# Half 0's frequency products in one piece, the router's input by transposing loads, and table 1's sine arguments on TensorE

## The chip, the cores and the metric

The kernel runs on one core of a Trainium2 chip. Its time is the device time of that core in microseconds (us), as the median of several runs. The engines are called as in the profile: PE (TensorE, matmuls), DVE (VectorE), ACT (ScalarE), POOL (GpSimd) and SP (SyncE, which issues most DMAs).

## The reference

For a sequence `x` of 2048 tokens and 512 channels the reference mixes a long convolution (branch a) and a small expert (branch b) with a gate per token:

```python
g = sigmoid((x * gate_w).sum(-1, keepdims=True))
a = _A_ref(x, A_re, A_im, B_re, B_im, C_re, C_im, log_dt, Dskip)
b = _B_ref(x, w_r, w_gate, w_up, w_down)
return g * a + (1 - g) * b

# _A_ref: a state space model as a convolution of length 2048
dt = exp(log_dt)[:, None]; logdA = dt * (A_re + 1j * A_im); dB = dt * Bc
l = arange(L).astype(bfloat16)
P = exp(logdA[:, :, None] * l)                      # 512 x 128 x 2048
K = einsum("dn,dnl,dn->dl", Cc, P, dB).real         # the kernel, 512 x 2048
y = irfft(rfft(K, padded) * rfft(u, padded))[:L] + u * Dskip

# _B_ref: the two tokens with the largest r get an expert's output
r = x @ w_r;  idx = argsort(-r)[:2]
y = (silu(x[idx] @ w_gate) * (x[idx] @ w_up)) @ w_down * sigmoid(r[idx])
return x + scatter(y at idx)
```

Inputs and output are bf16.

## The kernel before

**The method.** The lags `l` are rounded to bf16, so fewer distinct lags occur than there are tokens. The powers `P` are split in two tables of complex exponentials, table 1 (coarse lags, `tab1`) and table 2 (fine lags, `tab2`, with the weights folded in: the products r0 to r3). A matmul of the two over the 128 states gives the distinct values of the kernel (`kgen`, L920), selector matmuls sort them (`sel`, L933 to L949), and a matmul with constant matrices kp0 to kp4 turns them into the kernel's spectrum kk (`kspec`, L975). The sequence is cut in two blocks of 1024 tokens (0 and 1). A forward transform by matmuls with constant matrices f0 to f3 gives each block's spectrum X (`forward`, L896, evicted at L901; POOL's accumulating DMAs, L906, add the pairs `pm`). DVE multiplies spectra (`products`): block 1 of the output is X1*K0 + X0*K1, block 0 is X0*K0. The matrix g brings them back (`inverse`, L1057), and ACT or DVE scale the result by the gate and store it (L1068, L1072).

**Halves.** The 512 channels are worked on in two halves (h = 0, 1) of 256. Tables, kgen, kspec, products and inverse are done for each half, the forward transform once for both.

**Table 1's sines.** For a group g of up to four angles, `trig` scales the phase b16 once for each angle to a 32-bit integer tile `arg` (`SCL`, L477), takes the sine of its low 16 bits on ACT (`AC`, L463), adds a quarter turn to the tile (L667, DVE or ACT), and takes the sine again. Groups 0 and 1 have four angles, group 2 has two and gets the rest by doubling formulas, group 3 has none of its own.

**The router** (`routing`). Eight groups of eight transposes on PE (L766) bring u, 128 tokens by 128 channels at a time, to channel-major tiles xt0 to xt3, evicted by ACT or DVE through `EV` (L467). 64 matmuls with the gate's and the router's weights (L781) give the logits; four rounds of reductions (L796, L800) find the two largest; a gather matmul (L828), the expert's matmuls (L849, L863) and a small transpose (L870) follow. The result row zby is added to a copy of u in the output by an indirect DMA on POOL (L874), and u is loaded back from there before the inverse. xt lies where block 1's X comes later; w_down is loaded over xt once the logits are done.

**Products.** For a half, `products` is called four times: block 1 then 0, and in each the two halves of the frequencies (`qds` is (0,) or (1,)). A call makes one (block 0) or two (block 1) products of 4096 columns, adds them, and forms real and imaginary parts and the sum and difference over `pm` with pieces of 1024 columns, into X. The products lie in 8 KB tiles of the pools pqa, pqb, pqc and pqd.

**Order.** Nothing is scheduled at run time. Every operation has a number in the order in which the program states it. The string ORDER lists these numbers in the order in which they are put on their engines' queues; SECOND says for each operation that two engines can do which of them does it; PLACES gives PSUM banks and tiles. Each engine works its queue in order and waits by semaphores for what an operation reads or overwrites. DMAs of SP's queue are likewise in order: an issue that waits holds the ones behind it. ACT holds one of two function tables at a time; a change is a load of 1.28 us (L220).

**Places that matter here.** kp0 to kp3 lie over f0 to f3, so each can be loaded when the forward transform has used its f for the last time; kp4 lies behind them and is loaded near the start.

Of the kernel before, what the change touches and what calls it, by code (L numbers as in the profile page):

```python
# [10 lines left out]
F32 = mybir.dt.float32  # L11
# [342 lines left out]
def small_mats():  # L354
# [15 lines left out]
POOLS = {"pqa": 1, "pqb": 1, "pqc": 2, "pqd": 2}  # L370
ORDER = (
    "00k00500201601501l00000100300700d00h00i00400900600800u00g00e00c00j00f00n00l00m08e00o00p00q00s00r00t01g01d01e01h00x00y00z01c01801704003x04104801a01b03z"
    "04a03y01003v02502604900w00v01x01v01101208g04b01w01r01z04201y02002302402102701t05g01u04504301s02202804c01304604402902a02j02k05h03w02l02m02n01402o06k06j"
    "04d05i02p04e04705m05j02q02r05k05n01q04f02s03401o01p02b01j01m01i01902c01n01f02t06s02u03702v06r04i02w02x02y03802z06p03004j03103204l03303904k03c04g04m03d"
    "04h03i06l03a03504n06m08f04o03g03b06q06n06o04p03j04q05o04r03h02d04u04s03m06x06y04t06z07002e01k04w07107204y03n04v08i06t08j04z04x06u07300a03l07403k03o00b"
    "03p05007607505p08l05405305q06v06w05l07807706703q06605108v07907a08k05r05u05t05207c08m03r08s06808n08t03s03603t07d07b08u05507i07h07g07f07e07l07k06906a05v"
    "07j05905a05605b05c05x08w08h06b08x05d05708z08o05e05w05y08y08p09009t09v07m07p07n07o07q08q09o08r09107r09309n07s07t09207v02g09407u09p09w09509602h09709807z"
    "07y09q09u08107w09r09s0a10a20a308207x09x09y06c06d06005z0a40a50a60a80a70aa0a906e09z08c0a00ac0ab0ad0ae06g06f06108a06208d06308009a09905806h08308409b06402f"
    "08509e08603e09g03f0af08708b0ag0ai09c0aq0ah05s03u05f06506i09d0am09i09f0ar0b00b209j0880b10as0an0ak0aj0b30al0at0b70b80b90b40b50b60ax0ay0au0av09h09k0ap0ao"
    "09l09m0az0ba0be02i0c50890cd0bd0bb0bg0bh0aw0c60cc0c70c30c20c10bc0bk0bj0c00bi0bf0bl0dk0bm0bn0bp0bo0bq0dl0dh0bt0bu0br0bs0by0di0ce0c80bv0bw0cf0bx0d30d40cg"  # L380
    "0ct0c90c40ch0co0ca0dd0dg0bz0cv0cu0df0de0d50dj0ci0cb0cw0d00et0cj0dn0d60cq0cx0cp0d10d20do0dt0cy0cz0cl0eu0ck0d70du0da0dr0dp0dm0dq0d80dx0cr0d90e80db0dc0cm"
    "0cn0f30f40dv0ey0ez0dw0cs0ds0e40e70ea0ev0ew0e90ef0e30eb0ed0eh0el0ex0fs0f00fv0f50f10e50fo0e60fu0fr0fn0em0f70f60f20ec0eg0en0ee0ej0ft0fw0fx0fz0f80eo0g00g5"
    "0ek0ei0f90gh0fq0fp0fy0g30gi0fa0fb0fc0fd0g10ge0gd0g60gj0g70gl0dy0gf0gg0gk0gn0g80fe0gm0go0gq0g20g40dz0gp0ff0fg0fi0gr0fh0fj0h00gv0fm0fl0gw0gx0gy0fk0es0gs"
    "0gt0gu0er0ep0eq0e00gb0ga0gc0e20g90h10e10h90gz0ha0h40h50h60h20h70hb0h30h80hc"
)
SECOND = (
    "000000000000000000000000000000000000100000000000000000000000000000101010100010100000100100000000000000000000000000100010000000000000000000000010010001"
    "000110010100001010010010011010000000000000000000000000000000000000000000000000000000001010010010100000100000000000000000000000000000000000000000000000"
    "000001000001010000000100000110100000100100000000101000000010000010000000000000000000000000000000000000000000000000000000000000000000000000000000000000"
    "000000000000000000000000000000000000000000000000000000000000000000000000000000000000000000000000000000000000000000000000000000000000000000000000000000"  # L390
    "0000000000010011000100000"
)
PLACES = (
    "2406154064740000000020660011001266446040110064604014001100111016606022026424242200101026264262451016541026000171234265"
)
KB = 1024


def bass_gated_mix__ssm_conv_s4__moe_arch_mod__prompt_kernel(nc, A_u, A_A_re, A_A_im, A_B_re, A_B_im, A_C_re, A_C_im, A_log_dt, A_Dskip,
# [22 lines left out]
    with ExitStack() as es:  # L422
# [145 lines left out]
        for i in range(2, 6):  # L568
            prm_l(i, eng=ACT if i % 2 else SP)
# [583 lines left out]
```

## Time and profile before

| | |
|---|---|
| median of 3 runs (lowest to highest) | 153.71 us (153.7 to 154.03) |
| the profiled execution's own time | 153.72 us |
| its span, first to last instruction | 151.9 us |
| mean granted clock of PE | 0.955 |
| busy: PE, DVE, ACT, POOL | 129.7, 138.2, 131.1, 24.8 us |
| weight loads on PE | 96.4 us |
| DMA | 24.09 MB, mean 159 GB/s |
| start of kgen(0) on PE | 58.3 us after the span's start |
| start of kspec(0) on PE | 81.6 us |
| first product on DVE | 93.2 us |
| last matmul ends | 148.3 us |

Times within the span count from its start. "Busy" counts an engine's instructions from start to end, and neighbours overlap by some 0.09 us on DVE and ACT, so the cost of one more instruction in a full queue is its time from start to start, a little less than its mean duration. A row of a group gives line, engine, operation, shapes, how often it runs, its busy time and mean duration, and the idle time just before, with what ended it. A helper's line (L452, L467, L477) collects the operations of the whole kernel.

### The profile page before, as it was taken

To read this page: it belongs to the slowest core of one execution; us is meant where nothing else is said; L and a number is where in the kernel's file an instruction comes from. 1 tells how busy PE (TensorE), PEld (TensorE's weight loads), DVE (VectorE), ACT (ScalarE), POOL (GpSimd) and SP (SyncE) were. 2 spreads that over 40 slices of the span, in tenths; PEclk is the share of its full clock that TensorE was granted. 3 is DMA by queue.
4 is the path that set the end of the run, shared out by engine and by line. 5 is a ranking of instruction groups with operands and counts; after the bars stand their busy time and mean duration, and the time that the engine had idled before them with its cause. 6 is when DMAs were issued, how large, how long until landed. Compare 5 with 4: busy or idle time off the path is not lost.

```text
span 151.9 us, 3786 instructions
## 1 busy us (share of the span) xinstructions
PE 129.7 (85%) x1605; PEld 96.4 (63%) x1613; DVE 138.2 (91%) x199; ACT 131.1 (86%) x218; POOL 24.8 (16%) x17
## 2 busy tenths in 40 slices
PE   0974787467989986979996999997999999999990
PEld 0944542464354336973454787995888867888880
DVE  0499999999999999999999974999999999999961
ACT  3599999999999999999999569397599999999731
POOL 3000001000122999910055000001000000000000
PEclk9999999955699999999997799999999999999999
DMA  5999999939908604000389997006800001014154
GB/s 136 344 293 388 414 403 404 350 108 330 365 2 119 162 0 138 4 5 0 92 231 254 275 275 118 6 4 203 356 0 2 4 2 35 0 54 123 35 173 138
DMA packets 14546, 24.09 MB, mean 159 GB/s; under 512 B 1175, under 2 KB 10146, under 8 KB 14370
## 3 DMA queue, kind: packets, MB, share of 16 engines
q1 hardware_dynamic: 11410, 21.11, 40.8%
q0 software_dynamic: 2144, 2.10, 9.0%
q10 hardware_dynamic: 976, 0.66, 1.6%
q8 instruction: 12, 0.20, 0.5%
q14 instruction: 4, 0.03, 0.1%
HBM read 19.66 MB, written 4.20 MB: 157 GB/s over the span
## 4 chain that ended last, share of the span: by engine, by line
PE 53%; DVE 28%; ACT 8%; DMA 6%; issue 3%; SPq 0%; ACTq 0%
PE ps L1057 18%; DVE AR L452 18%; PE ps L975 13%; PE ps L920 11%; DMA AR<-c_ksp 4%; DVE AR L467 3%; ACT AR L463 3%; PE ps L896 2%; PE ps L1010 2%; DVE AR L477 2%; ACT AR L467 2%; ACT AR L667 2%; DMA AR<-c_bf 2%; DVE AR L456 1%; PE ps L933 1%
## 5 line engine op out<-in xcount | busy, mean ns | idle before, releaser
L452 DVE TENSOR_TENSOR AR<-AR 128x1024 bf16<-128x1024 bf16 (+8 forms) x129 | 115.6, 952 | 7.2 <-DMA AR<-c_bf 3.8
L467 ACT ACTIVATE AR<-ps 128x1024 bf16<-128x1024 f32 (+10 forms) x45 | 35.0, 807 | 9.1 <-PE ps L975 4.7
L896 PE MATMUL ps<-AR 128*128 128x512 bf16 x122 | 31.0, 405 | 3.2 <-ACT AR L901 1.5
L1057 PE MATMUL ps<-AR 128*128 128x256 bf16 x256 | 29.5, 273 | 0.0
L1057 PEld LDWEIGHTS ps<-AR 128*128 128x128 bf16 x256 | 25.0, 98 | 3.1
L896 PEld LDWEIGHTS ps<-AR 128*128 128x128 bf16 x128 | 12.5, 104 | 18.9 <-issue 3.6
L975 PE MATMUL ps<-AR 128*128 128x256 bf16 x160 | 20.8, 288 | 1.3 <-DMA AR<-c_ksp 1.3
L975 PEld LDWEIGHTS ps<-AR 128*128 128x128 bf16 x160 | 16.4, 103 | 5.3 <-DMA AR<-c_ksp 1.6
L920 PE MATMUL ps<-AR 128*128 128x84 bf16 (+1 forms) x512 | 17.9, 196 | 1.7 <-DVE AR L452 1.7
L920 PEld LDWEIGHTS ps<-AR 128*128 128x128 bf16 x512 | 17.8, 96 | 2.2 <-ACT AR L463 2.2
L463 ACT ACTIVATE AR<-AR 128x1024 bf16<-128x1024 int16 (+5 forms) x24 | 18.5, 773 | 0.5 <-DVE AR L477 0.3
L463 ACT ACTIVATE ps<-AR 128x256 f32<-128x256 bf16 (+1 forms) x36 | 18.0, 549 | 0.1
L874 POOL DMA_INDIRECT out_dram<-AR x1 | 16.2, 16210 | 2.8 <-ACT AR L477 2.8
L901 ACT ACTIVATE AR<-ps 128x1024 bf16<-128x1024 f32 x16 | 15.9, 1015 | 0.0
L1068 ACT ACTIVATE AR<-ps,AR 128x256 bf16<-128x256 f32 x28 | 11.4, 482 | 4.3 <-PE ps L1057 3.4
L477 ACT ACTIVATE AR<-AR 128x256 int32<-128x256 f32 (+2 forms) x28 | 13.8, 518 | 0.0
L463 ACT ACTIVATE AR<-ps 128x512 bf16<-128x512 f32 (+1 forms) x18 | 11.9, 757 | 2.0 <-PE ps L597 2.0
L906 POOL DMA_DIRECT2D AR<-AR x4 | 5.3, 1464 | 17.6 <-ACT AR L901 16.0
L667 ACT ACTIVATE AR<-AR 128x1024 int32<-128x1024 int32 (+1 forms) x9 | 7.8, 867 | 0.1
L766 PE MATMUL ps<-AR 128*128 128x128 bf16 x64 | 4.6, 220 | 3.2 <-DVE AR L452 1.4
L477 DVE TENSOR_SCALAR AR<-AR 128x256 int32<-128x256 f32 (+2 forms) x20 | 6.5, 336 | 0.0
L766 PEld LDWEIGHTS ps<-AR 128*128 128x128 bf16 x64 | 3.6, 98 | 4.3 <-DVE AR L467 2.0
(67 smaller groups left out, 91.3 us busy)
## 6 DMA issues: line engine op xcount, KB each, us to landing
AR<-c_ksp SPq DMA_DIRECT2D x5, 512.0 KB, 3.9
AR<-in_A_u_dram SPq DMA_DIRECT2D x4, 512.0 KB, 5.5
AR<-c_fwd SPq DMA_DIRECT2D x4, 512.0 KB, 7.9
AR<-AR POOLq DMA_DIRECT2D x4, 512.0 KB, 12.9
AR<-out_dram SPq DMA_DIRECT2D x4, 512.0 KB, 10.1
AR<-c_inv SPq DMA_DIRECT2D x1, 2048.0 KB, 8.8
AR<-in_B_w_up_dram SPq DMA_DIRECT2D x1, 1792.0 KB, 12.0
AR<-in_B_w_gate_dram SPq DMA_DIRECT2D x1, 1792.0 KB, 16.1
```

The lines of the kernel that those rows point to most:

```text
L452: return P.op(DVE, lambda h: h.tensor_tensor(out=o, in0=a, in1=b, op=op), rd, wr, cost=cst or tt_cost(o, a, b), **k)
L463: return P.op(ACT, lambda h: h.activation(out=o, in_=a, func=func, scale=scale, bias=bias), rd, wr, cost=0.185 + nel(o) * 0.833e-3 + (0.09 ...
L467: return P.op((ACT, DVE), (lambda h: h.activation(out=o, in_=a, func=ACTF.Copy), lambda h: h.tensor_copy(o, a)), rd, wr, cost=(0.185 + n * ...
L477: return P.op((ACT, DVE), (lambda h: h.activation(out=o, in_=a, func=ACTF.Copy, scale=c), lambda h: h.tensor_scalar(out=o, in0=a, scalar1= ...
L667: P.op((DVE, ACT), (lambda hh: hh.tensor_scalar(out=w, in0=w, scalar1=16384.0, scalar2=None, op0=ALU.add), lambda hh: hh.activation(out=w, ...
L874: P.op(POOL, lambda h: h.indirect_dma_start(dr(out, 0, (D, L), (1, D)), bass.IndirectOffsetOnAxis(ap=IDX(0, 2, 0, (1, 1)), axis=0), ZB(0, ...
L896: last = h.matmul(pb(0, 128, part * 512, (1, 512)), F[ft](0, 128, ((par * 4 + st) * 2 + part) * 128, (1, 128)), U(0, 128, (blk * 8 + st * ...
L901: P.op((ACT, DVE), (lambda hh, o=o, i_=i_, sc=sc: hh.activation(out=o, in_=i_, func=ACTF.Copy, scale=sc), lambda hh, o=o, i_=i_, sc=sc: hh ...
L920: last = hh.matmul(pb(0, 128, g // 6 * 512 + g % 6 * W4 + o, (1, n)), TP[h][1 - i // 2](0, 128, (b0 + g) * 128, (1, 128)), r[i](0, 128, (b ...
L975: last = hh.matmul(pb(0, 128, n * 256, (1, 256)), KP[u](0, 128, tau * 128, (1, 128)), KC[h](0, 128, jg * 256, (1, 256)), start=(k == 0 and ...
L1057: r = hh.matmul(pb(0, 128, e * 256, (1, 256)), G(0, 128, ((par * 2 + part) * 4 + ft) * 512 + (2 * t2 + e) * 128, (1, 128)), X(0, 128, blk ...
L1068: r = hh.activation(out=U(0, 128, tb * D + h * HC, (1, HC)), in_=pb(0, 128, e * 256, (1, HC)), func=ACTF.Copy, scale=SG(0, 128, 64 + tb, ( ...
```

## The change

- **Router input.** The eight transposes and their evictions go. Four DMAs on SP's queue load 128 channels each of u for all 2048 tokens, transposed on the way (`transpose=True`), straight into xt0 to xt3. The tokens now lie in their natural order, so the logit matmuls take every second column.
- **Table 1's sine arguments.** A new constant `an` (164 KB) holds the angles' multipliers, spread so that a matmul picks a channel's phase and multiplies it. The phases, reduced to one turn's fraction, are split on DVE (and for one step ACT or DVE) into two bf16 tiles pa0 and pa1. `angles` takes the place of `trig` in `tab1`: for each PSUM bank PE adds a rounding constant (512 columns), then eight matmuls of 128 columns written with stride 4; ACT takes the sine of the low 16 bits in PSUM; PE adds a quarter turn with one more matmul of 512 columns; ACT takes the second sine. Groups 0 and 1 need two banks each, group 2 one.
- **Places.** an, pa0 and pa1 lie where kp4 comes later, so kp4 is loaded after the last angles of half 1.
- **Products.** For half 0, `products` is called with both halves of the frequencies at once: two calls in place of four, with products of 8192 columns in 16 KB tiles (pools pqa and pqc with two units). Half 1 is as before.
- **New order.** ORDER, SECOND and PLACES are new. Read number by number: SP issues the parameters, `an`, the four transposing loads, then u's first quarter, f2, u's second quarter, f1, f3, u's other quarters, w_gate, w_up, half of w_down, the rest of the small constants, the other half, f0; later kp0, kp2, kp3, kp1, kp4 and the reloads of u. On PE the angles of groups 0 and 1 come first, then the logits, the angles of group 2, and the forward transform mixed with the router; half 1's angles of groups 0 and 1 stand between the expert's matmuls, its group 2 in the end of the forward transform. All four accumulating DMAs stand behind the indirect one on POOL. The last eviction of kgen(1) goes from ACT to DVE, behind the second product of half 0. Several other operations change engine or place.

```diff
-POOLS = {"pqa": 1, "pqb": 1, "pqc": 2, "pqd": 2}
+POOLS = {"pqa": 2, "pqc": 2, "pqd": 2}
...
+def angle_mats():
+    out = np.zeros((128, 642))
+    c = 0
+    for g in range(4):
+        j0 = DBL1.get(g, (4, 0, 0, 0))[0]
+        ts = [a // 8 for a in ANG1[4 * g:4 * g + j0]]
+        for i, t in enumerate(ts):
+            for p in range(128):
+                out[p, c + p % 64 * j0 + i] = t
+        c += 64 * j0
+    out[:, 640], out[:, 641] = 1.5 * 2.0 ** 23, 16384.0
+    return out
...
+        AN = B("an", oF + 16 * KB, 2 * 642)
+        PA = [B("pa%d" % i, oF + 16 * KB + 1536 + i * KB, 1 * KB) for i in range(2)]
...
+        DQ([(AN(0, 128, 0, (1, 642)), an_c[:, :])], [], [AN], 164352)
...
+        for db in range(4):
+            P.op(SP, lambda h, db=db: [h.dma_start(XT[db](0, 128, 0, (1, L)), dr(A_u, db * 128, (D, L), (1, 128)), transpose=True)], [], [XT[db]], cost=0.5, nbytes=786432, dma=True)
...
+        TS(DTC(0, 128, 0, (1, 4)), DTP(0, 128, 0, (1, 4)), -8.0 * c16, ALU.mult, [DTP], [DTC])
+        TT(XR[0](0, 128, 0, (128, 4), (1, 128)), PRM(0, 128, D, (128, 4), (1, 128)), DTC(0, 128, 0, (1, 4), (0, 128)), ALU.mult, [(PRM, 1), DTC], [XR[0]])
+        TS(f512(XR[1]), f512(XR[0]), MG, ALU.add, [XR[0]], [XR[1]])
+        STT(f512(XR[2]), f512(XR[1]), MG, f512(XR[0]), ALU.subtract, ALU.subtract, [XR[0], XR[1]], [XR[2]])
+        EV(f512(PA[0]), f512(XR[2]), [XR[2]], [PA[0]])
+        TT(f512(PA[1]), f512(XR[2]), f512(PA[0]), ALU.subtract, [XR[2], PA[0]], [PA[1]])
...
+        def angles(h, g, ts):
...
+            def add(hh, col, first):
+                for b in range(nb_):
+                    r = hh.matmul(pb(0, 128, b * 512, (1, w)), IDN(0, (1, 128)), AN(0, 128, col, (0, w)), start=first, stop=False, skip_group_check=True)
+                return r
+            def ang(hh):
+                add(hh, 640, True)
+                for x in range(2):
+                    for k in range(4):
+                        for b in range(nb_):
+                            r = hh.matmul(pb(0, 128, b * 512 + k, (4, w // 4)), PA[x](64 * h, 64, k * 128, (1, 128)), AN(64 * h, 64, c0 + b * (w // 4), (1, w // 4)),
+                                          start=False, stop=False, skip_group_check=True)
+                return r
+            so = lambda k: s(0, 128, k * 4 * HC, (16, 64), (1, 4 * na_))
+            P.op(PE, ang, [CBI, AN, *PA], [pb], cost=nb_ * (0.2157 + 8 * 0.1))
+            AC(so(0), lo, ACTF.Sin, [pb], [(s, "s")], scale=SC16, tset=ts)
+            P.op(PE, lambda hh: add(hh, 641, False), [CBI, AN], [pb], cost=nb_ * 0.2157)
+            AC(so(2), lo, ACTF.Sin, [pb], [(s, "c")], scale=SC16, tset=ts)
...
-                s = made[g] = trig(h, ANG1[4 * g:4 * g + j0], ts[g // 2], True, "1%d%d" % (h, g), 4) if j0 else place("snc", TRG, oI + 8 * KB, 6 * KB)
+                s = made[g] = angles(h, g, ts[g // 2]) if j0 else place("snc", TRG, oI + 8 * KB, 6 * KB)
...
-            for q in range(8):
-                bb = misc(True)
-                def tr(h, q=q, bb=bb):
...
-                P.op(PE, tr, uk(2 * q, 2 * q + 1) + [CBI], [bb], cost=0.455)
-                EV(XT[0](0, 128, q * 256, (2 * L, 2), (L, 2), (1, 256)), bb(0, 128, 0, (512, 2), (256, 2), (1, 256)), [bb], [(XT[i], q) for i in range(4)])
...
-                                last = h.matmul(b(0, 128, tb * 2, (1, 2)), XT[db](0, 128, tb * 128, (1, 128)), WL(0, 128, db, (4, 2)), start=(db == 0), stop=(db == 3))
+                                last = h.matmul(b(0, 128, tb * 2, (1, 2)), XT[db](0, 128, j * 1024 + st * 256 + par, (2, 128)), WL(0, 128, db, (4, 2)), start=(db == 0), stop=(db == 3))
...
-            for qd in range(2):
-                products(0, (qd,), (blk,))
+            for qds in (((0, 1),) if blk in (1, 0) else ((0,), (1,))):
+                products(0, qds, (blk,))
```

74 lines of the change are left out of this document (41 added, 33 removed).

## The prediction

> **What bounds the kernel now.** I read the slices first, to see which engine is full where, then the chain that ended last, then PE's and DVE's instructions in order of time, then the groups by shape for prices.
>
> The slices (one digit is 3.8 us):
>
> ```profile
> PE   0974787467989986979996999997999999999990
> DVE  0499999999999999999999974999999999999961
> ACT  3599999999999999999999569397599999999731
> PEclk9999999955699999999997799999999999999999
> DMA  5999999939908604000389997006800001014154
> ```
>
> DVE and ACT are full up to about 80 us while PE has gaps; from about 94 us PE and DVE are both full. PE's clock is halved once, around 31 to 41 us, and the DMA engines are full up to about 35 us. The chain, in its pieces:
>
> ```profile
> 50.44 7.76 DVE AR L452 x7
> ...
> 58.33 8.96 PE ps L920 x256
> ...
> 75.47 6.10 DMA AR<-c_ksp
> ...
> 81.61 8.83 PE ps L975 x64
> ...
> 107.22 7.09 PE ps L975 x64
> ```
>
> DVE builds half 0's table 2 until 58.2; PE then makes half 0's kernel (kgen, L920) until 67.3, finishes the forward transform at 75.45, and frees the forward matrix f1; kp1 is loaded over it (6.1 us); kspec(0) (L975) starts at 81.6, and from there PE runs almost without a gap to 148.3. So the end moves with the start of kspec(0), unless the products on DVE fall behind. PE before that, and the one long wait of DVE:
>
> ```profile
> 16.36 0.62 PE L766 MATMUL ps<-AR 128*128 128x128 bf16 x8
> 17.67 0.81 PE L896 MATMUL ps<-AR 128*128 128x512 bf16 x3 [0.69 <-DVE AR L467]
> 18.32 1.74 PE L781 MATMUL ps<-AR 128*128 128x2 bf16 x64
> 58.33 8.95 PE L920 MATMUL ps<-AR 128*128 128x84 bf16 x256 [1.73 <-DVE AR L452]
> 93.19 2.29 DVE L452 TENSOR_TENSOR AR<-AR 128x4096 bf16<-128x4096 bf16 x1 [2.92 <-DMA AR<-AR]
> ```
>
> Before kgen(0) PE waits for DVE; the products start at 93.2 when the accumulating DMA of block 1's X has landed.
>
> **Time base.** The profiled execution took 153.72 us, its span is 151.9, so 1.8 us lie around it; the median of the runs is 153.71, the same. A difference of 0.2% (0.3 us) is about what a measurement of this kernel tells from none.
>
> **Part 1, router input by transposing loads.** Removed: 64 transposes on PE (L766 back to back, 56 ns from start to start: 3.6 us), six evictions on DVE (0.69 us each, 0.60 from start to start: 3.6) and two on ACT (1.01, 0.95: 1.9). Added: four loads of 512 KB on SP's queue, ahead of u and the forward matrices. Their price is in no row, as no load here transposes. Lower bound: a plain 512 KB load, 1.35 us each when the loads stream (f2 lands at 12.58, u's next quarter at 13.93). By packets: a source row is 256 bytes, and packets of 256 bytes took 18 ns (136 of them) against 84 ns for 2048; 8192 packets of 18 ns on 16 engines are 9.2 us, 2.3 each. Upper end: the slowest 512 KB transfers of the trace, the accumulating ones, 5 us each when they share the engines. I take 2.3, since packet size is the property that a row shows; the loads would then land at about 14.5 (5.3, when the parameters and the angle constants are in, plus 9.2). SP issues nothing else meanwhile if it is held.
>
> The Trainium skill (VectorE: DVE Perf Modes, "The three transpose paths") gives the DMA path 1309 ns for a 128x128 block against 390 on TensorE, and tells authors to use TensorE where PSUM will do: it speaks against this part. An estimate from that figure: 64 blocks one after another 84 us, spread over 16 engines 5.2; no run here shows it.
>
> What waits: the logits (L781) stand in PE's new order behind the parameters' matmuls and the first angles, before any forward matmul, so a late landing stops PE. Behind the loads, u's quarters and f1 to f3 land 9.2 us later than they could, then w_gate (28.8 by sums of 4.7 us per 1.8 MB) and w_up (33.5), then w_down (38.7). In the new order PE comes to their matmuls at 30.6, 34.8 and 40.8, so some 2 us are spare.
>
> **Part 2, sine arguments by PE.** Removed: 20 scalings (5 on DVE at 0.28 us, 0.20 from start to start; 15 on ACT at 0.42, 0.33) and 6 quarter-turn adds (DVE 0.60; ACT 3 x 0.95 + 2 x 0.54): DVE -1.6, ACT -8.9. Added on DVE, once: a tiny scale, two arithmetic steps of 0.60, one of 0.36, a cast of about 0.45, a subtraction of 0.60: +2.7. Added on PE, per PSUM bank: two 512-column matmuls (0.216) and eight of 128 columns written with stride 4, as L597 writes (0.109 from start to start at full clock): 1.30 us; five banks per half, ten in all: 13.0. The sines themselves keep their size; ACT reads PSUM at the pace of SBUF (1042 against 1055 ns for 1024 columns).
>
> Sum of both parts, with the ops that change engine: DVE -2, ACT -11, PE +9.4. The load goes from the two full engines to the one that has gaps.
>
> **Where PE then stands.** From 10.0 to 58.3 PE was busy 37.2 us, 8.4 of it at half clock (4.2 at full). At full clock the same work is 33.0. New ahead of kgen(0) are half 0's five banks (6.5) and four banks of half 1 (5.2), gone are the transposes (3.6): +8.1, so 41.1. Waits along the new order, for sines, for the router's reductions on DVE and for eviction, add 3 to 6: kgen(0) starts at 54.4 to 57, I take 55.7. DVE's work up to its last table-2 product sums to 52.5, and the expert's result row (zby, waiting for dn at 42.4 and its transposes) holds it up about 2.5: 55.0. So the two meet, and kgen(0) starts 2.6 us earlier than 58.3. From there to the end of the forward transform is 17.1 as now plus the last angle group (1.1), less a little waiting: 73.7 instead of 75.45. kp1's landing (6.1, or some 5.0 by the selector matmuls that run meanwhile if kp4's later issue leaves kp1 freer) puts kspec(0) at 78.7 to 79.8: 2.3 us gained.
>
> kp4 moves from the first loads (it landed at 26.6) to behind kp1, since the angle constants lie in its place. Its 0.5 MB now runs beside the accumulating DMAs; kspec needs it 4.4 us after its start, by when it is in. POOL has all four accumulating DMAs behind the scatter now, with a memset among them; only one ran early before.
>
> **Part 3, products of half 0 in one piece.** 24 DVE instructions become 12 of twice the size: 12 fixed parts of 0.06 us (0.59 from start to start for 1024 columns, less 1024 x 0.523 ns) are 0.7 us of DVE. The price is order: the first product needs all of block 1's X and all four kk0 tiles (90.4 with kspec(0) at 79.8), where now one pair of kk0 tiles and half an X suffice. The accumulating DMAs move about 100 packets of 1 KB per us beside loads, 5.1 us for 512; from 75.5 the third lands near 91.5. So the products start at 91.5 instead of 93.2, the first 16 KB product takes 4.35 (2.285 + 4096 x 0.523 ns, less overlap). The last kgen(1) eviction is DVE's now, after the second product: at 101.5, no later than PE needs it. PE waits 1.0 us less there than now (1.4 at 102.2), of which I count 0.5. The inverse of half 0 then finds its X (pm add 109.8, pm sub 110.9) as PE gets there (110.9).
>
> **Sum.** -2.3 at kspec(0), -0.5 in the selector: 153.7 - 2.8 = **150.9 us**. By the ends of the waits, 148.9 to 153.
>
> **Rivals.**
> *Late transposes (slower).* From 16.5 us on, every us by which the transposed input lands later goes into PE's start, and from some 2 us beyond 14.5 also into w_up, w_down and zby. At 5 us per load they land at 25.3, 8.8 late: 159.7; halfway between my price and that (3.65) at 19.9: 154.3. For it: nothing in the trace bounds the write side of a transposing load; against: the packet sizes. No gain is left from a landing at 19.3 on (16.5 and the 2.8).
> *The accumulating DMAs decide.* Four of them, kp4 and the reloads of u share the engines from 73.7. For it: they ended DVE's wait at 93.2; against: the first is issued earlier now. If X of block 1 lands at 95 and that of block 0 at 100, the second product ends at 104.5, the eviction behind it holds the selector to 105, and the gain is lost: 153.7 to 154.5.
> *PE is not the bound (faster).* For it: PE had 11 us of gaps between 10 and 58.3; against: the sum above fills them. If PE's waits hide and DVE's saved 5.5 us (r3's last product 57.7 to 52.5) come through: 148.2.
> *The clock.* In the new order PE has only two short adds and the logits between 14.4 and 18.5. If the clock halves there for 10 us as it did from 30.7 to 41, PE loses 5 us, of which 2 fall in waits: about 154. The Trainium skill (TensorE: Matmul & The Clock Gate, "What's actually happening") says the clock halves after an idle window of about 3.4 us; the trace's halving at 30.7 follows 3 us in which PE ran mainly the gather.
>
> **Chances.** Forecast (149 to 153) 0.46; PE not the bound 0.12; late transposes 0.24; accumulating DMAs 0.10; clock 0.08. Of the last two somewhat under half still end below the bound. Faster 0.62, same 0.05, slower 0.33. The range leaves out transposes above 4.1 us each (150.9 + 5.1) and is 0.2 us below the faster case: 148.0 to 156.0; the forecast's own is 149 to 153.
>
> **What would show it.** Right: the transposing loads land by 16; PE's angle groups take about 2.2 us for two banks; kgen(0) starts near 55.7, kspec(0) near 79, the first 8192-column product near 91.5; ACT has gaps before 80. Wrong: a wait of the logits on a load of A_u beyond 17; half clock before 40 with PE busy; the first product waiting for an accumulating DMA past 93.

## The result and the profile after

The changed kernel takes 160.12 us (median of 4 runs, 159.48 to 160.79) against 153.7: a ratio of 1.0425, 95% interval 1.0368 to 1.0483. It is slower; 150.9 was forecast, in a range of 148 to 156. The profiled execution took 159.48 us with a span of 157.7, 5.8 more than before; 1.8 us lie around the span, as before. Runs of one kernel in which the granted clock was lower are several us longer; the ratios leave them out (where that leaves one run, there is no ratio), but the profiles of e2_evict, h1_front, h2_petr, j1_act and j2_act were taken in such runs, so places in time read from these five come out late.

The slices of the profile after (one digit is 3.9 us):

```profile
PE   2999809899999999999989998907999999999970
DVE  0899919999998999999999921999999999999960
ACT  3699992899979988899887785623499999998440
PEclk9999956999999999999999999985899999999998
DMA  4999999999777005200699999158000000010366
```

The load has moved as forecast: PE 137.1 us busy (129.7 before), DVE 136.6 (138.2), ACT 123.0 (131.1), and ACT now has gaps. But there are two holes. In slice 6 (19.7 to 23.7) PE and DVE wait together; later DVE waits (slices 24 and 25) and then PE (slices 27 and 28). PE's clock is at half from 19.7 to 26.5 and from 105.0 to 111.8. The chain that ended last names them; start, length, what:

```profile
3.53 2.98 SPq L601
...
15.23 7.84 DMA AR<-c_f
...
70.51 6.15 PE ps L941 x28
...
80.93 16.85 DMA AR<-AR
97.97 2.32 DVE AR L465
...
107.33 1.14 PE ps L978 x14
```

L601 is the transposing load, L941 the forward transform (L896 before), L978 the selector (L933). First the chain goes through SP's queue, held by the transposing loads, to the small constant c_f32, which the router's first spread matmul needs. Later it goes through an accumulating DMA. PE at the two places, with what ended each wait:

```profile
16.68 1.74 PE L826 MATMUL ps<-AR 128*128 128x2 bf16 x64
23.51 0.47 PE L845 MATMUL ps<-AR 128*128 128x128 f32 x1 [3.88 <-DVE AR L469]
23.77 1.91 PE L941 MATMUL ps<-AR 128*128 128x512 bf16 x4
...
107.33 1.14 PE L978 MATMUL ps<-AR 128*32 128x128 bf16 x16 [5.12 <-DVE AR L480]
```

And DVE:

```profile
23.17 0.29 DVE L469 TENSOR_SCALAR AR<-AR 128x128 f32<-128x128 f32 x1 [3.18 <-DMA AR<-c_f]
...
97.97 8.76 DVE L465 TENSOR_TENSOR AR<-AR 128x8192 bf16<-128x8192 bf16 x2 [6.17 <-DMA AR<-AR]
106.77 0.51 DVE L480 CAST AR<-ps 128x336 bf16<-128x336 f32 x1
```

The logits (L826) come at 16.7, near the forecast's 16.5; then DVE waits for c_f32 and PE for DVE. From 23.5 to 76.7 PE has no gap worth naming, so the late start goes through to the end of the forward transform. At 98 DVE starts the products, 6.2 us after it was free, and the last eviction of kgen(1), which the new order puts behind the second product, holds PE for 5.1 us.

Places in time (us from the span's start), with two kernels that are told of below: g0 is the changed kernel with two queues reordered; g1_plain is g0 with plain loads in place of the transposing ones and c_f32 ahead of them. It leaves out the transposing, so its logits are not the router's; only its times are used.

| | before | forecast | after | g0 | g1_plain |
|---|---|---|---|---|---|
| first spread matmul | 21.1 | | 23.5 | 23.2 | 19.9 |
| kgen(0) starts | 58.3 | 55.7 | 59.5 | 59.1 | 57.9 |
| forward ends | 75.4 | 73.7 | 76.7 | 76.7 | 75.4 |
| kspec(0) starts | 81.6 | 79.3 | 82.2 | 81.8 | 81.2 |
| first product of half 0 | 93.2 | 91.5 | 98.0 | 93.4 | 91.8 |
| kspec(1) starts | 107.2 | | 111.2 | 106.4 | 104.8 |
| last matmul ends | 148.3 | | 152.7 | 147.9 | 146.4 |
| span | 151.9 | 149.1 | 157.7 | 151.6 | 150.1 |

Of the 5.8 us, 0.6 are there at kspec(0) (where 2.3 were to be gained), 3.8 come between kspec(0) and the last matmul (66.7 us before, 70.5 after), 1.4 behind it (3.6 before, 5.0 after).

### The profile page after: what moved, and what is told of

Same layout as the page of the kernel before. It is cut to its first block, busy times and chain, and to the rows that moved or that the text cites. A ratio compares the mean times of both kernels' runs of the same rounds, so it can differ in the third digit from the quotient of the medians.

```text
span 157.7 us, 3818 instructions
## 1 busy us (share of the span) xinstructions
PE 137.1 (87%) x1638; PEld 103.2 (65%) x1649; DVE 136.6 (87%) x184; ACT 123.0 (78%) x193; POOL 15.3 (10%) x17
## 2 busy tenths in 40 slices
DMA packets 23011, 26.37 MB, mean 167 GB/s; under 512 B 9511, under 2 KB 18610, under 8 KB 22834
## 4 chain that ended last, share of the span: by engine, by line
PE 60%; DMA 16%; SPq 9%; DVE 8%; issue 2%; ACT 1%; POOL 0%; DVEq 0%
PE ps L1102 17%; PE ps L941 16%; DMA AR<-AR 11%; DVE AR L465 6%; PE ps L1020 6%; SPq L601 6%; PE ps L965 6%; DMA AR<-c_f 5%; SPq L493 3%; PE ps L717 3%; PE ps L1055 2%; PE ps L978 2%; PE ps L894 2%; PE ps L710 2%; PE ps L873 1%
## 5 line engine op out<-in xcount | busy, mean ns | idle before, releaser
L465 DVE TENSOR_TENSOR AR<-AR 128x1024 bf16<-128x1024 bf16 (+10 forms) x119 | 117.1, 1033 | 11.5 <-DMA AR<-AR 6.2
L480 ACT ACTIVATE AR<-ps 128x1024 bf16<-128x1024 f32 (+7 forms) x39 | 32.5, 853 | 15.2 <-PE ps L982 5.5
L941 PE MATMUL ps<-AR 128*128 128x512 bf16 x124 | 29.7, 390 | 0.3
L1102 PEld LDWEIGHTS ps<-AR 128*128 128x128 bf16 x256 | 25.0, 98 | 3.2
L476 ACT ACTIVATE AR<-ps 128x512 bf16<-128x512 f32 (+3 forms) x30 | 22.3, 804 | 2.8 <-PE ps L618 1.9
L941 PEld LDWEIGHTS ps<-AR 128*128 128x128 bf16 x128 | 12.7, 101 | 13.9 <-issue 1.2
L1020 PE MATMUL ps<-AR 128*128 128x256 bf16 x160 | 19.3, 275 | 0.7 <-ACT AR L480 0.7
L965 PEld LDWEIGHTS ps<-AR 128*128 128x128 bf16 x512 | 17.8, 96 | 0.9 <-issue 0.8
L1020 PEld LDWEIGHTS ps<-AR 128*128 128x128 bf16 x160 | 15.6, 99 | 3.9 <-ACT AR L480 0.9
L946 ACT ACTIVATE AR<-ps 128x1024 bf16<-128x1024 f32 x16 | 16.1, 1020 | 0.7 <-PE ps L941 0.6
L1113 ACT ACTIVATE AR<-ps,AR 128x256 bf16<-128x256 f32 x28 | 11.8, 483 | 4.3 <-PE ps L1102 4.1
L490 ACT ACTIVATE AR<-AR 128x256 int32<-128x256 f32 (+2 forms) x15 | 10.2, 687 | 0.4 <-DVE AR L465 0.4
L717 PE MATMUL ps<-AR 64*128 64x128 bf16 x80 | 9.8, 309 | 0.2 <-issue 0.2
L717 PEld LDWEIGHTS ps<-AR 64*128 64x128 bf16 x80 | 8.1, 130 | 2.3 <-issue 2.3
L978 PE MATMUL ps<-AR 128*32 128x128 bf16 x64 | 4.6, 422 | 5.1 <-DVE AR L480 5.1
L919 POOL DMA_INDIRECT out_dram<-AR x1 | 7.1, 7084 | 17.4 <-DMA out_dram<-in_A_u_dram 17.4
L476 ACT ACTIVATE AR<-AR 128x512 bf16<-128x512 int16 (+5 forms) x12 | 7.6, 630 | 0.6 <-DVE AR L465 0.5
L951 POOL DMA_DIRECT2D AR<-AR x4 | 5.2, 1580 | 15.8 <-ACT AR L946 15.8
```

The lines of the kernel that those rows point to most:

```text
L465: return P.op(DVE, lambda h: h.tensor_tensor(out=o, in0=a, in1=b, op=op), rd, wr, cost=cst or tt_cost(o, a, b), **k)
L476: return P.op(ACT, lambda h: h.activation(out=o, in_=a, func=func, scale=scale, bias=bias), rd, wr, cost=0.185 + nel(o) * 0.833e-3 + (0.09 ...
L480: return P.op((ACT, DVE), (lambda h: h.activation(out=o, in_=a, func=ACTF.Copy), lambda h: h.tensor_copy(o, a)), rd, wr, cost=(0.185 + n * ...
L490: return P.op((ACT, DVE), (lambda h: h.activation(out=o, in_=a, func=ACTF.Copy, scale=c), lambda h: h.tensor_scalar(out=o, in0=a, scalar1= ...
L717: r = hh.matmul(pb(0, 128, b * 512 + k, (4, w // 4)), PA[x](64 * h, 64, k * 128, (1, 128)), AN(64 * h, 64, c0 + b * (w // 4), (1, w // 4)) ...
L941: last = h.matmul(pb(0, 128, part * 512, (1, 512)), F[ft](0, 128, ((par * 4 + st) * 2 + part) * 128, (1, 128)), U(0, 128, (blk * 8 + st * ...
```

## The experiments

"First" and "second" sum of a block are the accumulating DMAs for its first and second half of the frequencies; u 1 to u 4 are u's quarters.

**e3_accum: POOL's order.**

```diff
-POOL: scatter, block 1 second, block 0 first, memset, block 1 first, block 0 second
+POOL: scatter, block 0 second, block 0 first, block 1 second, block 1 first, memset
```

> The changed kernel with one edit: on POOL's queue the two accumulating DMAs of block 0, whose X is evicted by 52.6 and 58.2 us, go ahead of those of block 1 (order: scatter, both of block 0, both of block 1, then the memset). Theory A (block 1's X is late because two transfers that could have run 15 us earlier share the engines with it): block 0's land before 70, block 1's at 86 to 90, the first 8192-column product starts at 91.8 when DVE is done with table 2 instead of 98.0, PE's wait of 5.1 us in front of sel(1) falls under 1, kspec(1) starts at 106 to 106.5, total 154.5 to 155.7. Rival S (the four loads of kp, the reloads of u and the sums share one rate, so the last sum lands when the bytes are done, at 97 or later, whatever the order): block 1's X at 94 to 97, total 157.5 to 159.5.

The profiled run took 155.44 us (span 153.6); there is no ratio, so g0 below, which has the same edit, has to bear this out. Block 0's sums land at 68.8 and 71.4, block 1's at 88.4 and 93.9; the first product starts at 94.1, kspec(1) at 107.4, and from kspec(0) to the last matmul it is 65.2 us instead of 70.5. Theory A, though block 1's second sum lands 4 us later than it said: two sums, kp and u together still share the engines after 76. POOL in the changed kernel, and then in g0:

```profile
76.53 2.67 POOL L951 DMA_DIRECT2D AR<-AR  x2 [15.80 <-ACT AR L946]
80.68 0.31 POOL L760 MEMSET AR<- 128x256 bf16 x1 [1.48 <-ACT AR L490]
80.93 2.58 POOL L951 DMA_DIRECT2D AR<-AR  x2
```

```profile
59.89 3.17 POOL L951 DMA_DIRECT2D AR<-AR  x2
76.51 1.27 POOL L951 DMA_DIRECT2D AR<-AR  x1 [13.44 <-ACT AR L946]
78.01 1.27 POOL L951 DMA_DIRECT2D AR<-AR  x1 [0.24 <-ACT AR L946]
```

In the first, POOL waits 15.8 us for the eviction that block 1's second sum needs, with a sum of block 0 behind it whose data were evicted by 58.2 and another, evicted by 52.6, last of all; then a memset that waits for ACT stands ahead of block 1's first sum. The four land at 87.0, 92.5, 97.8 and 100.3; the third is the one that the first product needs. It was issued at 80.9, 11.5 us before the one ahead of it landed, so nothing here shows that the memset cost anything.

**i2_bpool: that order alone, in the kernel before.**

```diff
-POOL: block 0 second, scatter, block 0 first, block 1 first, block 1 second, memset
+POOL: scatter, block 1 second, block 0 first, memset, block 1 first, block 0 second
```

> The kernel before with one edit: the changed kernel's order on POOL's queue (scatter, the second sum of block 1, the first of block 0, the memset, the first of block 1, the second of block 0) in place of its own (second sum of block 0 ahead of the scatter, then the rest). Theory A (that order by itself makes block 1's X late): the first product waits until 96 to 98 instead of 93.2, total 155.5 to 157.5. Rival M (the order is harmless in the kernel before, whose products need only half of X at a time, and costs only together with the 16 KB products): total 153.4 to 154.5.

158.61 us against 154.74: ratio 1.0196 (1.0116 to 1.0275). DVE:

```profile
96.87 2.29 DVE L452 TENSOR_TENSOR AR<-AR 128x4096 bf16<-128x4096 bf16 x1 [4.90 <-DMA AR<-AR]
```

kspec(0) to the last matmul is 70.0 us (66.7 before). Theory A; rival M falls: the order costs 3.3 us there by itself, without any 16 KB product.

**e2_evict: the eviction.**

```diff
-last eviction of kgen(1): DVE, behind the second product
+last eviction of kgen(1): ACT, behind the one before
```

> The changed kernel with one edit: the last eviction of kgen(1) goes from DVE, where it stands behind the second 8192-column product, back to ACT. Theory E (this eviction, for which PE waits 5.1 us at 107.3, is what the end hangs on): sel(1) starts at 103.6, kspec(1) at 107.4, total 156.2 to 156.8. Rival A (the products themselves are late, because X of block 1 lands at 97.8): sel(1) also starts at 103.6, but the inverse of half 0 finds its X no earlier than DVE's last sum for block 1, 116.3 instead of 116.8, so the wait only moves to the first inverse matmul: total 159.2 to 160.0.

Ratio 1.0359 (1.0230 to 1.0487), from runs of 159.22 and 161.19 us. In its profile the selector starts at 106.3 after a wait of 1.7 instead of 5.1, but PE then waits 2.05 us for DVE within kspec(1), and the inverse starts at 119.4 (117.2 after), the products at 99.6. From kspec(0) to the last matmul it is 70.8 us, no less than the 70.5 after. Rival A, though the selector is 2.7 us later than both theories said: the eviction's wait is only where the late products show first.

**e4_store: the output stores**, by the token tile and the half (t, h) that they begin with.

```diff
-SP: (10,0) (8,1) (14,0) (2,0) (10,1) (12,0) (12,1) (8,0) (0,0) (14,1) (6,0) (4,0) (0,1) (4,1)
+SP: (14,0) (12,0) (6,0) (4,0) (10,0) (8,0) (8,1) (10,1) (2,0) (0,0) (12,1) (14,1) (0,1) (4,1)
```

In the changed kernel (8,1), ready at 145.8, stands ahead of (14,0), ready at 133.6, and of (6,0), ready at 137.9.

> The changed kernel with one edit: the 14 output stores of SP's queue in the order in which their rows are ready. Theory T (stores of half 0 that were ready at 133 to 138 stand behind one that waits until 145.8, so SP issues to 155.2, 3 us after the last matmul): SP's queue ends at about 153.7, the span 1 to 1.5 us shorter, total 158.5 to 159.2. Rival (the last evictions and ACT's own two stores, issued to 154.2, set the end): total 159.5 to 160.2.

Ratio 1.0306 (1.0178 to 1.0435), so the total does not tell the theories apart: half clock lasts longer in its profile (18.8 to 29.0, and again twice), and the last matmul ends at 154.9. The tail does: 3.7 us from the last matmul to the end of the span, against 5.0 after and 4.7 to 5.1 in the three others. The step is as theory T has it; its worth of 1.3 us is read from the tail alone.

**g0: both orders together.**

> The changed kernel with the two queue orders tried before together: on POOL both accumulating DMAs of block 0 ahead of those of block 1, on SP the output stores in the order in which their rows are ready. It is the base for the next three. Theory A (the two are independent terms): profiled span of the first alone 153.6, less the 1.0 to 1.3 us of tail that the second saved: span 152.4, total 154.2, with kgen(0) still at 59 to 60 since the front is untouched. Rival C (what the order gained is lost again when TensorE's clock halves): the span varies with the granted clock between 152 and 157 from run to run, total up to 158.

154.67 us in ten runs against 153.79: ratio 1.0045 (0.9999 to 1.0091). Its profile (span 151.6, tail 3.7):

```profile
93.35 8.76 DVE L465 TENSOR_TENSOR AR<-AR 128x8192 bf16<-128x8192 bf16 x2 [1.56 <-DMA AR<-AR]
102.14 0.51 DVE L480 CAST AR<-ps 128x336 bf16<-128x336 f32 x1
```

The ratio falls from 1.0425 to 1.0045: nine tenths of the loss go with the order of two queues, and none of the three titled parts was touched. Theory A.

**g3_split: half 0's products in two pieces again.**

```diff
-            for qds in (((0, 1),) if blk in (1, 0) else ((0,), (1,))):
+            for qds in ((0,), (1,)):
```

> g0 with half 0's products in two halves of the frequencies again (each of the 12 large steps as two of half the size, one after the other, the half whose X lands first going first). Theory P (the size of these steps matters by their 12 fixed parts only, 0.7 us of DVE, and the first may start 1.5 us earlier since it needs half of X): the first product 1.5 us earlier than in g0, kspec(1) and the inverse within 1 us of g0's, total within 1 us of g0. Rival Q (16 KB steps delay whoever waits for the first half of them): total 1.5 to 3 us less than g0.

155.98 us, ratio 1.0136 (1.0053 to 1.0219). kgen(0) is 1.5 us later than in g0 for reasons that lie ahead of the edit; from kspec(0) to the last matmul it is 66.0 us, g0 66.2. The first product starts as soon as DVE is free, and the four take 8.95 us instead of two in 8.76. Theory P for this stretch, though the total is 1.3 us above g0's: the size of the pieces decides nothing here.

**e1_cf: c_f32 ahead of the transposing loads.**

```diff
-SP: an, xt2, xt0, w8, xt1, xt3, u 1, f2, u 2, c_f32, f1, f3, u 3, u 4
+SP: an, c_f32, xt2, xt0, w8, xt1, xt3, u 1, f2, u 2, f1, f3, u 3, u 4
```

> The changed kernel with one edit: the load of c_f32 goes ahead of the four transposing loads on SP's queue. Theory L (the late c_f32, which landed at 23.1 us, costs PE its 3.9 us wait and with it the gain ahead of kgen(0)): c_f32 lands by 8 us, the waits of DVE (3.2) and PE (3.9) are gone, kgen(0) starts at 56 to 57.5 instead of 59.5, kspec(0) at 79 to 80 instead of 82.2, and the accumulating DMAs, issued after the forward transform, end 2 to 3 us earlier; total 157.0 to 158.0. Rival F (the whole front of the DMA stream is late: u and f1 to f3 land at 24 to 28 whatever c_f32 does): the wait moves to the next load, kgen(0) at 59 or later, total 159.5 to 160.2.

Ratio 1.0468 (1.0362 to 1.0575). The spread starts at 21.1 instead of 23.5, but the first forward matmul right behind it waits 1.77 us for u and starts at 23.4; kgen(0) is at 60.3. Rival F: c_f32 was the last of several loads that all come late.

**g1_plain: plain loads**, c_f32 ahead of them as in e1_cf.

```diff
-h.dma_start(XT[db](0, 128, 0, (1, L)), dr(A_u, db * 128, (D, L), (1, 128)), transpose=True)
+h.dma_start(XT[db](0, 128, 0, (1, L)), dr(A_u, db * 128 * L, (L, 128), (1, L)))
```

> g0 with c_f32 ahead of the four transposing loads, and these made plain loads of the same 2 MB into the same tiles (the router's logits are then computed from untransposed rows; the rest is as it was). Theory T (the transposing loads hold SP's queue and the DMA engines to 16 us and so make u, f2 and the forward transform late, PE idles and its clock halves at 20 to 26): the four land by 11 us, u and f2 by 15, the first forward matmul at 21 to 21.7 instead of 23.9, no half clock before 30, kgen(0) at 55.5 to 57, total 150 to 151.8. Rival D (DVE's table 2, not PE, then holds kgen(0)): the front is early and kgen(0) still at 58 or later, total 153 or more.

151.45 us, ratio 0.9781 (0.9704 to 0.9857); by the ratios 2.6% less than g0. The four plain loads land at 13.8 (16.1 after), u's first two quarters and f2 at 15.1 to 17.7 (19.3 to 22.8). PE:

```profile
19.89 0.47 PE L845 MATMUL ps<-AR 128*128 128x128 f32 x1
20.16 1.91 PE L941 MATMUL ps<-AR 128*128 128x512 bf16 x4
22.02 0.48 PE L845 MATMUL ps<-AR 128*128 128x128 f32 x1
22.29 3.60 PE L941 MATMUL ps<-AR 128*128 128x512 bf16 x8
...
33.21 3.90 PE L941 MATMUL ps<-AR 128*128 128x512 bf16 x11 [0.24 <-issue]
```

The wait is gone, and theory T has the time right but not the way: eight forward matmuls take 3.60 us instead of 1.89, at half clock, though PE did not wait before them, and eleven later ones 3.90 instead of 2.54. The clock is at half from 18.9 to 25.7 and from 32.6 to 36.0. So kgen(0) is at 57.9, not 55.5 to 57: without a wait that took 3.1 us in g0 and 3.9 after, it is only 1.2 and 1.6 us earlier.

**h1_front, j1_act, j2_act, g2_fwd1st: can the loads be had cheaper?** All four start from g0.

```diff
-g0, SP:       an, xt2, xt0, w8, xt1, xt3, u 1, f2, u 2, c_f32, f1, f3, u 3, u 4
+h1_front, SP: an, w8, c_f32, xt2, xt0, xt1, xt3, u 1, f2, u 2, f1, f3, u 3, u 4
+g2_fwd1st, SP: an, c_f32, u 1, u 2, f2, xt2, xt0, f1, w8, xt1, xt3, f3, u 3, u 4
+j1_act, SP:   w8, c_f32, xt2, xt0, u 2, f2, xt1, xt3, f1, f3, u 3;  ACT: an, u 1, u 4
+j2_act, SP:   an, w8, c_f32, xt2, xt0, xt1, xt3, f1, f3, u 3, u 4;  ACT: u 1, u 2, f2
```

> g0 with c_f32 and the two small loads of the router's weight w8 ahead of the four transposing loads, so that these follow each other without a plain load between. Theory B (a plain load between two transposing ones costs about 1.3 us: 3.2 us from the second landing to the third in the changed kernel, 1.8 to 1.9 between the others): the four land by 14.6 to 15.2, u and f2 by 20.4, first forward matmul at 21.5 to 22 instead of 23.5, kgen(0) at 57.3 to 58.5, total 1 to 2 us less than g0 (152.7 to 153.7). Rival (transfers take turns at the same rate whatever their order): last landing at 16 or later, kgen(0) within 0.5 us of g0, total 154.2 to 155.

The four landed at 10.3, 12.5, 15.3 and 17.2: the expectation's theory B is wrong, they take 2.0 to 2.7 us each without a plain load between them, and the last landing is the rival's. The first forward matmul waits 1.9 us for u and starts at 23.2. There is no ratio; one run took 156.14 us.

In g2_fwd1st the first eight forward matmuls also go ahead of the logits on PE.

> g0 with c_f32, u's first two quarters and f2 ahead of the four transposing loads (f1 between them), and on PE the first eight forward matmuls ahead of the logits. Theory T as in g1: forward starts at 17 to 18, the logits at 20.5 to 22 when the last transposing load lands, PE idles under 2.5 us between 10 and 26 instead of 4 and keeps its clock, kgen(0) at 56.5 to 58, total 151.5 to 153. Rival R (the router is the longer chain): logits 4 to 5 us later push gather, expert and scatter back, PE waits at the spread or the gather for what it saved, kgen(0) at 59 to 61, total 154 to 156.

164.08 us, ratio 1.0650 (1.0587 to 1.0713). Rival R, and worse. SP's queue shows why:

```profile
5.51 10.00 SPq L601 DMA_TRANSPOSE AR<-in_A_u_dram  x2
...
16.91 6.62 SPq L601 DMA_TRANSPOSE AR<-in_A_u_dram  x2
```

The first transposing load was held on SP until 13.2, when f2 landed (13.3), the third until 20.9, when f1 and w8, which I had left between them, landed (20.9 to 21.4). The logits came at 29.0.

j1_act and j2_act issue plain loads from ACT's queue. j1_act moves other loads than its expectation says (the list above is what it did), with plain loads between the transposing ones on SP.

> g0 with c_f32 and w8 ahead of the four transposing loads on SP, and the first two quarters of u and f2 issued from ACT's queue at about 8 us instead of from SP's behind the transposing loads. Theory N (only SP's queue is held; plain loads of another queue use what the transposing ones leave): u, f2 land by 17 to 19.5 instead of 19.3 to 22.9, the last transposing load by 18, logits at 18 to 19, first spread at 21 to 22, first forward matmul right behind it, kgen(0) at 57.5 to 58.7, total 152.8 to 154. Rival S (the DMA engines themselves are full while they transpose, so what u gains the transposing loads lose): u and f2 land at 19 to 22, logits at 19.5 or later, spread at 22.5 or later, kgen(0) at 59 or later, total 154.5 to 157.

Ratio 1.0182 (1.0108 to 1.0257); the third transposing load was held from 11.9 to 20.4, when f2 was about to land (20.55).

> The edit that j1_act was meant to make (there the angle constants and two other quarters of u went to ACT's queue, and plain loads stood between the transposing ones on SP): g0 with c_f32 and w8 ahead of four uninterrupted transposing loads on SP, and u's first two quarters and f2 issued from ACT's queue at about 8 us. Theory N (only SP's queue is held): u, f2 land by 17 to 19.5, the last transposing load by 18, first spread at 21 to 22 with the forward right behind it, kgen(0) at 57.5 to 58.7, total 152.8 to 154. Theory S (the engines are full, or a transposing load waits for plain ones in flight, as in j1_act, where one was held on SP from 11.9 until f2 landed at 20.55): the third and fourth transposing loads land at 19 or later, logits at 20 or later, kgen(0) at 60 or later, total 155 or more.

Ratio 1.0226 (1.0119 to 1.0334). ACT issued its loads at 5.5 to 6.9, and with these in flight the first transposing load landed at 19.3 instead of 9.2, u 1, u 2 and f2 at 16.7 to 19.5, the third transposing load at 23.8. Theory S: it isn't SP's queue, the two kinds of load get in each other's way.

**h2_petr, i1_petr: part 1 undone** in g0, with the router's loops of the kernel before, in two places of PE's queue (q 0 to 7 are its eight groups, fwd eight forward matmuls).

```diff
-SP: an, xt2, xt0, w8, xt1, xt3, u 1, f2, ...
+SP: an, w8, c_f32, u 1, u 2, f2, u 3, u 4, f1, ...
+h2_petr, PE: q0, angles g0, g1, q1, q2, q3, turn g0, q4, q5, q6, q7, w8, turn g1, logits, angles g2
+i1_petr, PE: angles g0, g1, w8, q1, q2, turn g0, q3, q4, turn g1, q5, fwd, q6, q7, q0, angles g2, logits
```

> g0 with part 1 undone: no transposing loads; the router's input is transposed on PE from u's tiles (64 transposes, 8 evictions, 6 on DVE and 2 on ACT) in the new order, and u, f2 and c_f32 are loaded first. Theory W (PE, with part 2's sine arguments, is now the bound of the front, so the 3.6 us of transposes come back in full while the loads' 4 to 5 us are saved): kgen(0) at 58 to 60, total 153 to 155, about g0's. Rival T (the loads cost more than the transposes, which find place in PE's waits before 20 us): kgen(0) at 56 to 57.5 and total 150.5 to 152, as with the plain loads.

> g0 with part 1 undone once more, the transposes now placed behind the two large angle groups, in two PSUM banks, half of their evictions on ACT, with the first eight forward matmuls between them; no transposing loads, u, f2 and c_f32 loaded first. Theory W (PE bounds the front; the dense forward matmuls among the transposes keep its clock, and the wait of 2 to 4 us for u goes): first forward matmul at 17 to 19, logits at 20.5 to 22.5, no half clock before 32, kgen(0) at 56 to 58, total 150.5 to 152.5. Rival V (the transposes wait for their evictions one by one, as in the first try): logits at 24 or later, kgen(0) at 60 or later, total 155 or more.

h2_petr: no ratio, 157.41 us in one run; in its profile the logits come at 30.8, so it fits neither theory. i1_petr: ratio 1.0438 (1.0383 to 1.0492), logits at 27.1, kgen(0) at 67.8. Rival V there: the transposes wait for their evictions and the router's chain is 7 us late or more at the spread (30.5). These two price my placements and not part 1, whose cost without the loads stays open; g1_plain gives only the price of transposing on the way.

**h3_fill: more work for the clock**, on h1_front.

```diff
-PE: turn g0, turn g1, logits, angles g2, spread
+PE: turn g0, turn g1, 4 unread matmuls, logits, angles g2, 8 unread matmuls, spread
```

> h1_front with 12 matmuls of 128x512 added on PE whose result nobody reads: 4 ahead of the logits, 8 behind the first one-bank angle group, where PE waits. Theory K (the clock halves at 20 to 26 because PE does little between 14.7 and 23, short adds, two-column logits and a wait; the halving then costs the forward matmuls 1.5 to 3 us): with the fill the granted clock stays over 0.9 from 20 to 32, kgen(0) 1 to 2.5 us earlier than in h1_front, total 1 to 2 us less. Rival (the clock halves on the load of PE as a whole, or on something else): half clock at 20 to 26 as before, the added work costs up to 1 us, total as h1_front or up to 1.5 us more.

157.62 us, ratio 1.0167 (1.0042 to 1.0292). The granted clock and PE's busy time from 20 to 26 us, in the changed kernel, in h1_front and in h3_fill (start to end, length, busy, clock, DMA share, GB/s):

```profile
20.00:26.00 6.00, 2.49 (x7) 0.50 1.04 401
```

```profile
20.00:26.00 6.00, 3.67 (x11) 0.50 1.01 367
```

```profile
20.00:26.00 6.00, 5.68 (x23) 0.72 1.01 378
```

The half clock got shorter (20.3 to 23.7, in h1_front 20.0 to 26.9), but most of the second fill ran in it (eight matmuls in 3.10 us), and kgen(0) is at 59.5, as in the changed kernel. The total is the rival's: the fill costs at least what it gains.

## Why the prediction was wrong, point by point

**Time base, engine sums.** 1.8 us around the span: held. PE +7.4 (forecast +9.4), ACT -8.1 (-11), DVE -1.6 (-2): right in sign, and within 3 us in size. A two-bank angle group took 2.2 to 2.5 us and its quarter turn 0.6 (2.6 forecast for both).

**The transposing loads.** 2.3 us each was right: from 6.72, when `an` landed, to 16.12 are 2.35 each. Their start was not: `an` was in at 6.7, not 5.3. It cost nothing at the logits, 16.7, so the rival "late transposes" did not happen as written. The profile's page counts 9511 packets under 512 bytes, 1175 before: the loads do move in pieces of a source row, as the price assumed. The Trainium skill (DMA: Bandwidth & Descriptors, "Latency and other measured facts") gives transposing DMAs 261 GB/s with a non-contiguous middle dimension, and some 350 to 400 in the contiguous case. An estimate by 261 is 8.0 us for the 2 MB; the changed kernel took 9.4, or 223 GB/s.

**The step that failed first: what stands behind them.** I listed u, f1 to f3 and the weights as late but "some 2 us are spare", and did not see that c_f32 is in the same queue between u's second quarter and f1 (the list of SP's queue ahead of the prediction does not show it there either), or that the router needs it right after the logits. That is a wait of 3.9 us on PE (19.6 to 23.5) for which the sum had no term. e1_cf shows that PE would have waited for u otherwise; g1_plain that the wait goes with the transposing loads. The lateness then goes through PE's whole queue: the first weight matmuls come at 34.4 (30.6 forecast), dn runs from 44.7 to 46.3 (40.8 to 42.4), DVE's last table-2 product ends at 59.3 instead of 55.0, and PE's forward matmuls ahead of kgen(0) at 59.5. The two do meet, 3.8 us later than forecast. Nor were 2 us spare: the weights landed at 33.8, 38.4 and 43.7, 5 us later than forecast, 0.1 to 1.1 us before PE came to them.

The rest of that stretch came out right in part by luck. From 10 to 59.5 us PE waited 5.7 us in all, within the 3 to 6 of the sum, since its other waits were only 1.8. It was busy 43.8 us, of which some 1.5 are the price of the half clock; the other 42.3 stand against 41.1 forecast.

**The clock.** Given 0.08 and 154 us, for PE doing little but short adds and the logits: this is what happened. The clock was at half from 19.7 to 26.5, in part while PE waited, and cost those 1.5 us before kgen(0), 1.2 of them in the first twelve forward matmuls (4.1 us instead of 2.9). It is not the wait that set it off, for it begins with the wait: in the 3.4 us before 19.7 PE was busy 3.2 us, mostly with the 64 logit matmuls of two columns (1.74 us) and eight matmuls of 64 rows (1.04). In g1_plain it halved at 18.9 without a wait of PE over 0.4 us since 14.7, and as PE had work then, it lost more: from 18.4 to 26.0 PE was busy 7.5 us at a clock of 0.55. In h3_fill it halved for less time when PE did more. The Trainium skill (TensorE: Matmul & The Clock Gate, "What's actually happening") says that the clock halves after an idle window of about 3.4 us. The second halving, at 105.0, is close to that, with PE idle from 102.2; the first does not agree, unless matmuls of few columns or rows count as next to idle. What sets it off is not settled here.

The prediction says that the clock halves once in the kernel before. Its PEclk row shows a second dip, in slices 22 and 23: 0.50 from 82 to 84 us and 0.66 from 84 to 86, at the start of kspec(0). By these figures some 1.7 us (an estimate) of the 66.7 from kspec(0) to the last matmul are clock; g0, with 1.00 from 80 to 88, does not pay them. So its 66.2 against 66.7 shows no gain from the new products or the new order.

**kgen(0) to kspec(0).** 17.1 us to the forward's end (18.0 forecast), 5.5 to kspec(0) (5.0 to 6.1): held.

**The step that failed most: the accumulating DMAs.** I had written that all four are behind the scatter, "with a memset among them", and took the third at 91.5: some three times 5.1 us from 75.5. It landed at 97.8. 1.0 us of that is the later issue (76.5). The rest is the first sum, which took not 5.1 but 10.5 us from issue to landing, in company with kp and u; the second and third followed 5.5 and 5.3 us apart, near the price. The kernel before had shown this: its first late sum was issued at 76.2 and landed at 88.0, and 5.1 us is only the distance from there to the next landing (93.1). The rival "the accumulating DMAs decide" has this mechanism; I gave it 0.10, with X1 at 95, X0 at 100 and the selector held to 105: it was 97.8, 100.3 and 107.3. And I did not ask whether the order had to be so: block 0's data were there at 52.6 and 58.2 and POOL was free at 60.7, but its sums were issued at 77.3 and 81.7. g0 shows that the other order brings the first product to 93.4, and i2_bpool that this order has its price without the new products.

**The eviction.** "At 101.5, no later than PE needs it": 106.8, because it hangs on the products. With the products on time (g0) it starts at 102.1 and PE waits 0.8, near the forecast's 0.4.

**The tail.** No term for it: 1.4 us, of which the order of the stores makes 1.3 (3.7 us in e4_store and g0).

**Sum.** 2.9 at kspec(0), 4.3 between there and the last matmul (3.8 lost instead of 0.5 gained) and 1.4 in the tail make 8.6 between the forecast span and the real one. With the two orders mended and the loads plain it is 151.45 us, near the forecast of 150.9, but by luck: kspec(0) starts at 81.2 there and not at 79.3, and 65.2 us instead of the forecast's 66.2 follow. With the transposing loads the kernel is no better than before. No run undoes part 2, so what the sine arguments on PE are worth by themselves stays open.

## What to carry to other kernels

When a change brings a new order, read every queue of it number by number and ask of each entry what it waits for and what ready work stands behind it: here two sums on POOL and a row of stores, neither of them part of the change's aim, were worth 5.7 us, twice the aim's 2.8. Moving one constant, whose wait was as plain in the profile, gained nothing, since u stood right behind it. A price that is right for a transfer is not yet the price of the queue that it heads. And a rival whose mechanism one can already see in the order deserves its arithmetic carried to the end, not a tenth.

## What the runs showed of the hardware

- A transposing load does not stream behind plain ones: its issue is held on SP until the loads ahead on the queue have landed or nearly so (13.2 against 13.3 in g2_fwd1st, 20.4 against 20.55 in j1_act, 6.5 against 6.7 after), and three plain ones of 512 KB in flight from another queue stretched the first from 5.7 to 14.6 us from issue to landing (j2_act).
- Behind the last transposing load the first two plain loads of 512 KB took 5.4 us to land (16.1 to 21.5; in g0 4.1, from 17.1 to 21.2); plain loads that stream take 1.3 each (g1_plain).
- The accumulating DMAs of 512 KB landed 2.7 us apart when little else ran (68.3 and 71.0 in g0) and 5.3 to 5.5 apart beside kp and u; the first of such a row took 10.5 from issue to landing (11.8 before).
